# A new order of the same operations in a fused attention and feed-forward kernel

## The chip, the core and the metric

The kernel runs on one core of one Trainium2 chip. Its time is the device time of that core in microseconds (us), the median of several runs: 196.02 us before the change (three runs, 195.33 to 196.46). Apart from these runs one execution was profiled. It took 195.43 us, 193.5 us of it from the first to the last instruction (the span); the granted TensorE clock was 0.977 on average.

## What is computed

Two parts follow each other: an attention through 32 inducing points, and a feed-forward layer with x - tanh(x) in the middle.

```python
B, N, m, C = (4, 12480, 32, 128)
def mab(q, kv):
    s = scale * (q @ kv.transpose(0, 2, 1))
    s = s - s.max(-1, keepdims=True)
    a = np.exp(s)
    a /= a.sum(-1, keepdims=True) + 1e-09
    return a @ kv
h = mab(I, x)          # 32 inducing rows attend to the 12480 rows of a batch
x = mab(x, h)          # the 12480 rows attend to the 32 rows of h
...
h = x @ w_in           # 128 -> 2048
g = h - np.tanh(h)
return (g @ w_out).astype(np.float32)
```

All is float32. The output has 49920 rows of 128 numbers.

## The kernel before

**Tiling.** Each of the 4 batches is cut into 8 full segments of 1536 rows and one rest of 192 rows. A segment is written here as batch.segment, so 3.7 is the last full segment of the last batch and 3.8 is its rest. A full segment is 768 KB.

**First pass, for each batch.** The transposed segment is loaded (L383, `in_xT` into a `big` tile). TensorE multiplies it with the inducing rows (`scores`, L360 with `indT_sb`; called S1 here), and VectorE copies the scores out of PSUM and takes their maximum (L394). When all segments of a batch are through, the greatest score is found (L407 on VectorE, L409 on TensorE, L411, L417, and L420, which writes its negative `nbs`). Then comes, for each segment, the exponential on ScalarE (L468), a transpose of its 32x32 blocks on VectorE (L472, tile `et`), and the accumulation with the rows of x (L479; called ACC). ACC needs the segment with rows on the partitions. That layout comes in one of two ways: it is loaded from a second array (L462, `in_xn`), or, for the segments listed in `TURNED`, TensorE transposes it from the tile already there in three groups of four (L454; called T), and ScalarE or VectorE moves each group out of PSUM (L458). Batch 3 has two groups of segments (`GROUPS`): 3.0 and 3.1 are accumulated with a first greatest score, the others with the final one.

**Between the passes.** From the accumulated rows, `linear` works out for each batch the product with the two weight matrices to first order (L532, L356, L592), which leaves a small matrix `P_all` for each batch. A branch at the end goes to an exact form where the inputs are too large for this; it isn't taken here. The weights arrive as 64-bit words and are unpacked early in the program (L314 to L336: load, two steps on ScalarE, three on VectorE, two on GpSimd for each of 8 pieces).

**Second pass, for each segment.** S2 (L360 with `hT_all`) makes the scores, VectorE their maximum over 32 (L619, L620), ScalarE the exponential (L623), TensorE the product with `P_all` (L630; called prod). VectorE takes the sums out (L642) and inverts them (L645). The four quarters of the result leave PSUM either on VectorE, already scaled (L654), or on ScalarE unscaled (L658), after which GpSimd scales them in SBUF (L663). Then the segment is stored (L689). `DVQ` says how many quarters prefer VectorE.

**What sets the order.** No order is written by hand. `Plan.order` replays the list of operations with a cost for each, five engines and limited places: 23 `big` tiles, 8 PSUM banks and so on. An engine that is free takes the ready operation with the smallest priority number; the priorities are worked out from the table `K` (one number per batch and kind of operation, plus a step per segment). Each engine's instructions are then emitted in the order of this replay, and which tile an operation gets is settled by it too. At run time each engine takes its instructions strictly in that order. All DMAs, loads and stores, are issued by SyncE (SP) from one such queue, so a DMA that waits for its tile or its data holds back every DMA behind it. A load into a `big` tile waits until the last reader of that tile has finished: for a tile that held a transposed segment this is the segment's S2, for a tile with the other layout its ACC, for a result tile its store.

`LEAD`, `AHEAD`, `ISSUE` and `LAND` are the replay's DMA times, `SWITCH` and `STAY` its price for a change of TensorE mode, `MOST` limits how many `big` tiles one kind may hold.

Of the kernel before, what the change touches and what calls it, by code (L numbers as in the profile page):

```python
# [28 lines left out]
K = dict(load=(-307.0, -11.8, 121.4, 497.6), step1=(166.6, 10.8, 57.6, 54.7), lag2=(-1203.5, -373.8, -119.7, 417.3),
         copy=(-1617.1, 506.9, 485.8, -141.8), step2=(87.9, 64.9, 8.6, 29.9), turn=(1778.8, 1519.9, 3008.9, 2697.8),  # L30
         move=(-990.8, 721.0, 514.0, -475.8), nat=(-1233.4, 238.3, -127.2, -13.2), exp1=(-625.3, -464.9, 2706.6, 1215.5),
         et=(-962.3, 167.1, 1061.9, -1333.0), acc=(-504.7, 258.7, -313.0, -2258.1), sc2=(38.1, -215.7, -836.8, 1739.2),
         top=(1608.0, 619.3, 675.7, 692.4), exp2=(225.9, 24.6, 1508.1, -1683.1), prod=(-936.2, 1846.7, -190.5, 507.5),
         rec=(-1896.3, -404.8, 830.2, 246.0), ev=(1184.4, 55.1, 422.6, -1850.0), off=(-135.0, 428.4, 1368.7, 1417.9),
         step3=(99.8, 177.4, 103.4, 154.9), w1=-51.2, w2=1048.6, bound=2406.7)
# [868 lines left out]
```

## Time and profile before

| | |
|---|---|
| median of three runs | 196.02 us |
| the profiled execution | 195.43 us, of it 193.5 us span |
| TensorE (PE) busy | 159.4 us, 82% of the span |
| VectorE (DVE) busy | 149.1 us, 77% |
| ScalarE (ACT) busy | 113.0 us, 58% |
| GpSimd (POOL) busy | 96.8 us, 50% |
| moved by DMA | 67.26 MB, 41.17 MB read and 25.56 MB written |

In the profile's lines, PE stands for TensorE's matmuls and PEld for its weight loads. An L with a number is a line of the kernel. A group of instructions is written as engine, line, operation, output and input tile with shapes, and how many there were. A time in square brackets behind a row of the timeline is how long the engine stood idle just before it, and what it was released by; "issue" there means that it waited for nothing that the profile shows. A float32 matmul leaves two records, so an S1 or S2 of four matmuls counts as x8, an ACC as x24, a prod as x24; a group T of four transposes counts as x4.

### The profile page before, as it was taken

Reading aid. Unit: us, or ns where it says so; the run is one execution under the profiler, and the core shown is the slowest. Engines: PE = TensorE matmul, PEld = TensorE weight load, DVE = VectorE, ACT = ScalarE, POOL = GpSimd, SP = SyncE. Lnnn points to the kernel's source line nnn. Section 1 sums busy time; section 2 is a strip of 40 time slices with the busy share of each in tenths; the row PEclk is TensorE's granted clock in tenths of the full one; section 3 lists DMA queues with packets and bytes.
Section 4 is the critical chain, followed back from the end, with each engine's and each line's share of the span. In section 5 each row is a group of like instructions: output and inputs, shape, how many; then the busy total and the mean of one; then the engine's idle time right before and its main releaser. Section 6 shows DMA issues by size and latency. Waiting matters only on the chain.

```text
span 193.5 us, 7184 instructions
## 1 busy us (share of the span) xinstructions
PE 159.4 (82%) x2809; PEld 101.7 (53%) x2809; DVE 149.1 (77%) x556; ACT 113.0 (58%) x283; POOL 96.8 (50%) x117
## 2 busy tenths in 40 slices
PE   0799958686989969989999899997999996999500
PEld 0555647433466746546757675562776564565300
DVE  3277799979988858796799866993997679888950
ACT  3013399942289934766779924641797673588700
POOL 4000207645420547488544434432437995399980
PEclk9999999999999999999999999999999999999955
DMA  5999996999999999999999999999699995648893
GB/s 150 410 424 412 406 334 207 361 418 419 417 417 377 318 338 414 354 407 403 378 357 340 335 422 418 341 370 410 230 332 418 414 376 198 238 166 344 357 391 86
DMA packets 14201, 67.26 MB, mean 348 GB/s; under 512 B 1745, under 2 KB 2897, under 8 KB 14161
## 3 DMA queue, kind: packets, MB, share of 16 engines
q1 hardware_dynamic: 14160, 66.74, 90.2%
q8 instruction: 24, 0.39, 0.8%
q14 instruction: 17, 0.13, 0.2%
HBM read 41.17 MB, written 25.56 MB: 345 GB/s over the span
## 4 chain that ended last, share of the span: by engine, by line
PE 55%; DVE 13%; DMA 12%; ACT 8%; issue 5%; POOL 3%; SPq 0%; DVEq 0%; POOLq 0%; ACTq 0%
PE ps L360 17%; PE ps L630 13%; PE ps L454 10%; PE ps L479 8%; DMA big<-in_xT 7%; DMA big<-in_xn 5%; POOL big L663 3%; ACT ex L623 2%; ACT s L468 2%; PE ps L356 2%; ACT big L458 2%; ACT big L658 2%; PE ps L532 2%; DVE big L323 1%; DVE mb L619 1%
## 5 line engine op out<-in xcount | busy, mean ns | idle before, releaser
L663 POOL TENSOR_TENSOR big<-big,mb 128x384 f32<-128x384 f32 (+1 forms) x68 | 71.8, 1082 | 49.6 <-ACT big L658 41.0
L658 ACT COPY big<-ps 128x384 f32<-128x384 f32 x95 | 40.6, 491 | 10.8 <-DVE S_all L642 9.9
L630 PE MATMUL ps<-P_all,ex 32*128 32x129 f32 (+1 forms) x784 | 37.7, 292 | 3.1 <-issue 2.2
L630 PEld LDWEIGHTS ps<-P_all,ex 32*128 32x128 f32 (+1 forms) x784 | 29.5, 184 | 18.8 <-issue 8.0
L360 PE MATMUL ps<-big,indT_sb 128*32 128x384 f32 x256 | 27.7, 507 | 10.8 <-DMA big<-in_xT 8.3
L623 ACT ACTIVATE ex<-ps,mb 128x384 f32<-128x384 f32 (+1 forms) x36 | 20.2, 566 | 21.4 <-DVE mb L620 11.6
L458 ACT COPY big<-ps 128x512 f32<-128x512 f32 x30 | 17.3, 598 | 25.4 <-PE ps L454 24.9
L454 PE MATMUL ps<-ident,big 128*128 128x128 f32 x216 | 31.0, 288 | 0.0
L479 PE MATMUL ps<-big,et 128*32 128x128 f32 x768 | 27.0, 275 | 4.4 <-DVE et L472 3.1
L454 PEld LDWEIGHTS ps<-ident,big 128*128 128x128 f32 x216 | 24.2, 145 | 12.1 <-issue 5.3
L360 PE MATMUL ps<-big,hT_all 128*32 128x384 f32 x256 | 27.6, 491 | 1.5 <-issue 1.4
L479 PEld LDWEIGHTS ps<-big,et 128*32 128x32 f32 x768 | 20.8, 110 | 10.5 <-DVE et L472 5.1
L394 DVE TENSOR_SCALAR_CACHE_REDUCE s<-ps 128x384 f32<-128x384 f32 (+1 forms) x36 | 18.3, 518 | 10.1 <-PE ps L360 8.9
L642 DVE TENSOR_SCALAR S_all<-ps 128x3 f32<-128x3 f32 (+1 forms) x136 | 13.5, 154 | 10.7 <-PE ps L630 10.1
L619 DVE TENSOR_REDUCE mb<-ps 128x1 f32<-128x384 f32 (+1 forms) x36 | 18.4, 510 | 4.1 <-PE ps L360 3.6
L468 ACT ACTIVATE s<-s,nbs 128x384 f32<-128x384 f32 (+1 forms) x36 | 21.1, 608 | 0.0
L472 DVE STREAM_TRANSPOSE et<-s 128x384 f32<-128x384 f32 (+1 forms) x36 | 18.3, 525 | 1.6 <-ACT s L468 1.0
L458 DVE COPY big<-ps 128x512 f32<-128x512 f32 x24 | 16.4, 689 | 2.9 <-PE ps L454 2.5
L654 DVE TENSOR_TENSOR big<-ps,mb 128x384 f32<-128x384 f32 x33 | 17.6, 543 | 0.7 <-PE ps L360 0.2
L317 POOL TENSOR_SCALAR big<-big 128x512 f32<-128x512 f32 x8 | 5.3, 687 | 19.3 <-DMA big<-in_w_in 19.3
L360 PEld LDWEIGHTS ps<-big,indT_sb 128*32 128x32 f32 x256 | 6.1, 110 | 16.2 <-issue 7.5
L360 PEld LDWEIGHTS ps<-big,hT_all 128*32 128x32 f32 x256 | 6.9, 109 | 8.9 <-issue 5.1
(122 smaller groups left out, 159.4 us busy)
## 6 DMA issues: line engine op xcount, KB each, us to landing
big<-in_xT SPq DMA_DIRECT2D x32, 768.0 KB, 9.5
out<-big SPq DMA_DIRECT2D x30, 768.0 KB, 6.2
big<-in_xn SPq DMA_DIRECT2D x14, 768.0 KB, 9.3
big<-in_w_in SPq DMA_DIRECT2D x4, 512.0 KB, 12.8
big<-in_w_out SPq DMA_DIRECT2D x4, 512.0 KB, 10.3
out<-big SPq DMA_DIRECT2D x4, 384.0 KB, 3.1
xr<-in_xT SPq DMA_DIRECT2D x4, 96.0 KB, 8.8
xnr<-in_xl SPq DMA_DIRECT2D x4, 96.0 KB, 9.7
```

Source lines behind the costliest of these rows:

```text
L360: nc.tensor.matmul(ps[q * m:(q + 1) * m, :sg], lhsT=w, rhs=seg(x, nq, None, q), start=True, stop=stop)
L394: nc.vector.tensor_scalar(out=s1.get()[:P, :sg], in0=ps.get()[:P, :sg], scalar1=1.0, scalar2=None, op0=ALU.mult, op1=ALU.max, accum_out=mx ...
L454: nc.tensor.transpose(out=ps.get()[:, k * 128:(k + 1) * 128], in_=xt.get()[:, c:c + 128], identity=ident)
L458: copy(x.get()[:, 4 * g:4 * g + 4, :].rearrange("p k c -> p (k c)"), ps.get())
L468: nc.scalar.activation(out=t, in_=t, func=AF.Exp, bias=nbs.get()[:P, g:g + 1], accum_out=sums.get()[:P, s:s + 1])
L472: add("DVE", 0.5 if s < NS else 0.25, lambda et=et, s1=s1s[s], P=P, sg=sg, kb=kb: nc.vector.transpose(out=et.get()[:P, :kb].rearrange("p k ...
L479: nc.tensor.matmul(hacc.get()[q * m:(q + 1) * m, g * C:(g + 1) * C], lhsT=et.get()[:P, k, :], rhs=x.get()[:P, k, :], start=first_k[g, q] = ...
L619: nc.vector.tensor_reduce(out=mb.get()[:P, 0:1], in_=ps.get()[:P, :sg], axis=AX.X, op=ALU.max)
L623: add("ACT", 0.49 if full else 0.28, lambda: nc.scalar.activation(out=ex.get()[:P, :sg], in_=ps.get()[:P, :sg], func=AF.Exp, bias=mb.get() ...
L630: nc.tensor.matmul(o_b[q].get()[:T, r * (C + 1):(r + 1) * (C + 1)], lhsT=ex.get()[p, r * T:(r + 1) * T], rhs=P_all[p, b, :], start=True, s ...
L658: nc.scalar.copy(out=slot(q, q + 1), in_=o(q)[:, :, :C])
L663: nc.gpsimd.tensor_tensor(out=x, in0=x, in1=mb.get()[:T, 2 + q0 * nr:2 + q1 * nr].unsqueeze(2).to_broadcast([T, w, C]), op=ALU.mult)
```

## The change

Only numbers are changed, and one priority that was tied to another (`pri - 200`) becomes a number per batch in `K`.

```diff
-LEAD, AHEAD, ISSUE, LAND = 1.5, 4.0, 0.35, 1.5
-SWITCH, STAY = 0.115, 92.5
-MOST = dict(xT=15, xn=15, ot=21, pm=13)
-K = dict(load=(-307.0, -11.8, 121.4, 497.6), step1=(166.6, 10.8, 57.6, 54.7), lag2=(-1203.5, -373.8, -119.7, 417.3),
...
+LEAD, AHEAD, ISSUE, LAND = 1.50, 2.50, 0.35, 1.35
+SWITCH, STAY = 0.115, 138.5
+MOST = dict(xT=15, xn=14, ot=44, pm=24)
+K = dict(load=(-491.1, 150.9, 186.6, 689.9), step1=(131.5, 25.1, 45.2, 4.2), lag2=(-1155.7, -401.5, -325.5, 647.7),
...
-TURNED = ((0, 1, 2, 3, 4, 5, 6, 7), (2, 4, 6), (1, 2, 4, 5, 7), (4, 7))
+TURNED = ((0, 1, 2, 3, 4, 5, 6, 7), (1, 2, 4, 6), (1, 2, 4, 5, 7), (4,))
...
-DVQ = ((0, 3, 3, 1, 1, 2, 0, 0, 1), (0, 2, 1, 2, 1, 0, 1, 1, 1), (1, 0, 1, 3, 0, 0, 2, 1, 1), (2, 1, 2, 1, 2, 1, 2, 3, 0))
+DVQ = ((2, 3, 1, 2, 3, 1, 0, 2, 1), (1, 1, 2, 1, 0, 1, 0, 2, 1), (2, 0, 1, 3, 2, 0, 1, 1, 1), (1, 1, 2, 0, 0, 2, 2, 3, 0))
...
-                out=dst[:, q0 * nr:q1 * nr, :], in_=slot(q0, q1)), reads=[ot, *pieces[q0:q1]], pri=pri - 200)
+                out=dst[:, q0 * nr:q1 * nr, :], in_=slot(q0, q1)), reads=[ot, *pieces[q0:q1]], pri=pri + K["st"][b])
```

The count of operations of each kind on TensorE and of DMAs stays the same: 18 segments are transposed on TensorE before and after, and 14 are loaded in the second layout. One of them changes sides: 1.1 was loaded and is now transposed, 3.7 was transposed and is now loaded. Of the 136 quarters of the second pass, 31 instead of 33 full ones leave PSUM on VectorE and 97 instead of 95 on ScalarE, and GpSimd scales them in 70 instead of 68 pieces.

The first place is TensorE's row around the greatest score of batch 1, up to the first accumulation of that batch. Before, all transposes of batch 1 stand ahead of these rows; L409 and L417 are the greatest score's two steps, L592 and L356 belong to batch 0's `linear`, L360 is S1 of 2.0 and L479 the ACC of 1.0:

```order
L454 MATMUL ps_179<-ident,big_266 128x128 x4
L454 MATMUL ps_130<-ident,big_266 128x128 x4
L409 MATMUL ps_144<-ident,mx 1x128
L592 MATMUL ps_165<-wout_sb,W_627 32x128 x16
L417 MATMUL ps_137<-one,row 32x1 x4
L356 MATMUL ps_157<-P_753,foldx 32x128 x4
L360 MATMUL ps_172<-big_94,indT_sb 32x384 x4
L479 MATMUL ps_144<-big_252,et_372 32x128 x12
```

The same place now:

```order
L409 MATMUL ps_149<-ident,mx 1x128
L454 MATMUL ps_142<-ident,big_226 128x128 x4
L454 MATMUL ps_128<-ident,big_282 128x128 x4
L592 MATMUL ps_170<-wout_sb,W_631 32x128 x16
L417 MATMUL ps_177<-one,row 32x1 x4
L360 MATMUL ps_149<-big_86,indT_sb 32x384 x4
L454 MATMUL ps_135<-ident,big_282 128x128 x4
L356 MATMUL ps_157<-P_759,foldx 32x128 x4
L454 MATMUL ps_142<-ident,big_282 128x128 x4
L479 MATMUL ps_128<-big_338,et_372 32x128 x12
```

Four of the transposes (the last group of 1.4 and the three of 1.6) moved behind the start of the search for the greatest score, between its steps; the three groups of 1.1 are new and stand further ahead.

The second place is SP's row where batch 3's second layout is loaded. Before, xn 3.0 and 3.1 come first, then xT 3.7, then the stores of 1.3 to 1.5, then xn 3.2, 3.3, 3.5, 3.6 and the rest's, then stores again:

```order
L462 DMA big_177<-in_xn 128x1536
L462 DMA big_252<-in_xn 128x1536
L383 DMA big_94<-in_xT 128x1536
L689 DMA out<-big_266 128x1536
L689 DMA out<-big_226 128x1536
L689 DMA out<-big_342 128x1536
L462 DMA big_252<-in_xn 128x1536
L462 DMA big_266<-in_xn 128x1536
L462 DMA big_336<-in_xn 128x1536
L462 DMA big_342<-in_xn 128x1536
L462 DMA xnr_308<-in_xl 64x384
L689 DMA out<-big_319 128x1536
```

The same place now, from xT 3.7 on: xn 3.0, the store of 1.4, then xn 3.1, 3.2, 3.3, 3.5, 3.6 and 3.7 in a row, the rest's, and only then the store of 1.5:

```order
L383 DMA big_252<-in_xT 128x1536
L462 DMA big_86<-in_xn 128x1536
L689 DMA out<-big_126 128x1536
L462 DMA big_313<-in_xn 128x1536
L462 DMA big_133<-in_xn 128x1536
L462 DMA big_126<-in_xn 128x1536
L462 DMA big_155<-in_xn 128x1536
L462 DMA big_349<-in_xn 128x1536
L462 DMA big_133<-in_xn 128x1536
L462 DMA xnr_769<-in_xl 64x384
L689 DMA out<-big_200 128x1536
```

The loads of xn 3.0 and 3.1 moved behind xT 3.7, xn 3.7 is new and takes the tile that xn 3.2 had (`big_133`), and the store of 1.5 moved behind them all. By the tiles that they take, xn 3.0 now waits for S2 of 2.0, 3.1 for S2 of 2.1, 3.2 for S2 of 2.2, 3.3 for the store of 1.4, 3.5 for S2 of 2.3, 3.6 for S2 of 2.4 and 3.7 for ACC of 3.2.

The third place is VectorE's row between batch 3's final greatest score (L420) and the first block transpose that depends on it (L472, segment 3.2). Before, with two of the moves of 3.7 (L458) between them:

```order
L420 TENSOR_SCALAR nbs<-ps_172 128x1
L458 COPY big_226<-ps_157 128x512
L425 TENSOR_REDUCE nmx<-nbs 128x1
L458 COPY big_226<-ps_144 128x512
L472 STREAM_TRANSPOSE et_389<-s_142 128x384
```

Now:

```order
L420 TENSOR_SCALAR nbs<-ps_142 128x1
L645 RECIPROCAL mb_741<-S_all 128x12
L425 TENSOR_REDUCE nmx<-nbs 128x1
L654 TENSOR_TENSOR big_313<-ps_177,mb_741 128x384
L472 STREAM_TRANSPOSE et_410<-s_140 128x384
```

The two moves are gone, and a reciprocal and one quarter of 2.1 stand there instead.

From L532 of batch 3 (the start of its `linear`) to the end of the program TensorE has the same operations in the same order before and after, but for two pairs of rows that change places; GpSimd has the same from L582 of batch 3 on.

More of the change, by code (lines that the diff above doesn't have):

```diff
@@ L25 @@
 SMALL = 0.0625
-LEAD, AHEAD, ISSUE, LAND = 1.5, 4.0, 0.35, 1.5
-SWITCH, STAY = 0.115, 92.5
-MOST = dict(xT=15, xn=15, ot=21, pm=13)
-K = dict(load=(-307.0, -11.8, 121.4, 497.6), step1=(166.6, 10.8, 57.6, 54.7), lag2=(-1203.5, -373.8, -119.7, 417.3),
[L30 to L35, printed above, removed]
-TURNED = ((0, 1, 2, 3, 4, 5, 6, 7), (2, 4, 6), (1, 2, 4, 5, 7), (4, 7))
+LEAD, AHEAD, ISSUE, LAND = 1.50, 2.50, 0.35, 1.35
+SWITCH, STAY = 0.115, 138.5
+MOST = dict(xT=15, xn=14, ot=44, pm=24)
+K = dict(load=(-491.1, 150.9, 186.6, 689.9), step1=(131.5, 25.1, 45.2, 4.2), lag2=(-1155.7, -401.5, -325.5, 647.7),
+         copy=(-1436.1, -91.7, 401.2, 866.6), step2=(53.0, 21.8, 29.6, 11.2), turn=(2464.2, 1619.9, 3834.7, 2397.6),
+         move=(-1235.8, 1620.0, 792.5, -1062.6), nat=(-88.4, 388.6, 263.4, 221.6), exp1=(-761.0, -1191.3, 3121.8, 1092.9),
+         et=(-1743.8, -396.7, 697.9, -989.9), acc=(-415.6, 311.0, -914.8, -2852.2), sc2=(397.9, -270.3, -981.4, 1175.3),
+         top=(1314.2, 389.7, 382.8, 391.6), exp2=(699.1, 100.5, 1581.4, -1536.3), prod=(-1389.7, 1876.4, 309.4, 838.7),
+         rec=(-1614.8, -1055.1, 943.4, 458.0), ev=(1578.9, 169.1, 83.6, -1972.7), off=(-434.6, 597.2, 1423.8, 1605.1),
+         step3=(98.7, 160.5, 133.8, 209.3), st=(-638.4, -255.5, -294.7, 320.5), w1=-629.9, w2=752.2, bound=2143.0)
+TURNED = ((0, 1, 2, 3, 4, 5, 6, 7), (1, 2, 4, 6), (1, 2, 4, 5, 7), (4,))
 GROUPS = ((0,), (0,), (0,), (0, 2))
-DVQ = ((0, 3, 3, 1, 1, 2, 0, 0, 1), (0, 2, 1, 2, 1, 0, 1, 1, 1), (1, 0, 1, 3, 0, 0, 2, 1, 1), (2, 1, 2, 1, 2, 1, 2, 3, 0))
+DVQ = ((2, 3, 1, 2, 3, 1, 0, 2, 1), (1, 1, 2, 1, 0, 1, 0, 2, 1), (2, 0, 1, 3, 2, 0, 1, 1, 1), (1, 1, 2, 0, 0, 2, 2, 3, 0))
 LOADED = [(b, s) for b in range(4) for s in range(8) if s not in TURNED[b]]
```

## The prediction

> **What bounds the kernel now.** I read the page first, for the shares (the table above), then the stretches, to see where each engine fills, then the timeline of TensorE and VectorE at the stretches that aren't full, then how long DMAs took from issue to landing.
>
> ```profile
> core 0: us, PE busy (x) PEld busy (x) DVE busy (x) ACT busy (x) POOL busy (x), PEclk, DMA share, GB/s
> 24.00:30.00 6.00, 3.24 (x45) 2.60 (x46) 5.88 (x17) 5.38 (x13) 1.34 (x2) 1.00 0.86 291
> 42.00:48.00 6.00, 4.70 (x72) 2.19 (x68) 5.76 (x18) 1.61 (x4) 2.59 (x2) 1.00 1.02 421
> 48.00:54.00 6.00, 5.61 (x55) 2.44 (x56) 5.93 (x18) 1.67 (x3) 2.50 (x3) 1.00 1.01 414
> 96.00:108.00 12.00, 12.00 (x210) 7.90 (x206) 11.07 (x41) 10.13 (x29) 5.28 (x5) 1.00 0.99 329
> 138.00:145.00 7.00, 6.94 (x144) 5.29 (x147) 6.58 (x23) 6.56 (x22) 3.63 (x3) 1.00 0.85 268
> ```
>
> No engine bounds the whole. TensorE has the most work, 82% of the span, but from 24 to 54 us VectorE is the full one (5.88, 5.76 and 5.93 of 6 us) while TensorE waits, and from 42 to 54 us the DMAs run at their highest rate too, 414 to 421 GB/s. From 96 to 108 us TensorE is full while DMA gives only 329 GB/s. A new order removes no work, so it can win only where TensorE stands idle and has work that could be moved there, or lose where a load comes too late.
>
> One part can be set aside. From L532 of batch 3 on the order is the same, and that stretch is long:
>
> ```profile
> 154.17 1.39 PE L532 MATMUL ps<-win_sb,hT_all 128*32 128x512 f32 x8
> ```
>
> 193.5 - 154.2 = 39.3 us. So the change has to act ahead of 154 us, and I count its terms as shifts of this L532. The prices of TensorE's pieces come from the chain and the timeline:
>
> ```profile
> 11.18 1.46 PE ps L454 x12
> 60.19 0.88 PE ps L630 x24
> 61.86 0.65 PE ps L360 x8
> 62.50 0.65 PE ps L479 x24
> 86.95 0.87 PE ps L592 x32
> 88.70 0.36 PE ps L356 x8
> 98.15 0.31 PE ps L409 x2
> 54.42 1.57 ACT big L458 x3
> ```
>
> So a transposed segment is 1.46 us on TensorE, a prod 0.88, an S1 or S2 0.65, an ACC 0.65; the two parts of `linear` are 0.87 and 0.36, the steps of a search for the greatest score about 0.3. Moving a transposed segment out costs ScalarE 1.57.
>
> **Term 1: 1.1 is transposed, 3.7 is loaded.** Up to L532 of batch 3 TensorE's sum stays the same; 1.46 us move from after 136 us to before 59 us. What matters is whether they fit into idle time there.
>
> ```profile
> 51.13 0.85 PE L360 MATMUL ps<-big,indT_sb 128*32 128x384 f32 x8 [0.19 <-DVE wout_sb L332]
> 52.94 0.85 PE L360 MATMUL ps<-big,indT_sb 128*32 128x384 f32 x8
> 58.10 0.43 PE L356 MATMUL ps<-P,foldx 128*32 128x128 f32 x8 [0.76 <-ACT P L595]
> 59.32 0.86 PE L479 MATMUL ps<-big,et 128*32 128x128 f32 x24 [0.15 <-DVE et L472]
> ```
>
> S1 of 1.6 starts at 51.13 and S1 of 1.7 at 52.94. The load of 1.7 took this long:
>
> ```profile
> 34.30 5.01 SPq L383 DMA_DIRECT2D big<-in_xT  x4
> big<-in_xT SPq DMA_DIRECT2D x1, 768.0 KB, 13.5
> ```
>
> It was the last of those four, issued at about 39.0, and landed at 52.5, right before its S1. At 418 GB/s (between the rates above) 768 KB are 1.9 us, and in the new row of SP the load of xn 1.0 no longer stands ahead of the xT of batch 1. So 1.7 can land about 1.9 us earlier, at 50.6. Of the new row between S1 of 1.7 and ACC of 1.0, TensorE has 9 groups of transposes (9 x 1.46 / 3 = 4.4 us), the two parts of `linear` (1.2), S1 of 2.0 (0.65) and the search's steps (0.3), 6.6 us, and I count 7 for the changes between them. From an end of S1 at about 51.5 this is done at 58.5, ahead of 59.32. And ACC of 1.0 waits for the search and the exponential, which hang on VectorE:
>
> ```profile
> 55.24 0.12 DVE L407 TENSOR_REDUCE mx<-mxg 128x1 f32<-128x9 f32 x1
> 57.56 0.16 DVE L420 TENSOR_SCALAR nbs<-ps 128x1 f32<-128x1 f32 x1
> ```
>
> VectorE has the same work ahead of L420 in both orders (L407 goes ahead of one maximum, the others stay), so L420 and the ACC come at about the same time, but by then TensorE has done the transposes of 1.1 on top of all that stood ahead of this ACC before. If it fits, the term is -1.46 us. If 1.7 lands no earlier, the row ends at 53.7 + 7.0 = 60.7, 59.32 is passed by 1.3 us, and the term is -0.2. I take -1.2, since the DMA rate there is steady. The moves of 1.1 are all ScalarE's, which is busy only 1.6 of 6 us there; without that cover they would add 1.57 us.
>
> **Term 2: xT 3.0.** TensorE waited for it:
>
> ```profile
> 101.19 9.62 DMA big<-in_xT
> 110.94 0.85 PE L360 MATMUL ps<-big,indT_sb 128*32 128x384 f32 x8 [0.87 <-DMA big<-in_xT]
> ```
>
> It is issued when S2 of 1.5 has freed its tile. Before, 8.1 us of TensorE's work (six groups T, four ACC, two prod, one S2 and the same S1) lay between that S2 and S1 of 3.0; now it is 6.3 us (five ACC, two prod, one group T, one S2 and the rest's small S1). The load itself now follows the other DMAs around it by some 4 us more, and 96 to 108 us had DMA to spare, so it should take less than 9.62 us. At the 7.4 us of a load that stood alone in SP's row (123.43, below) TensorE waits 1.1 us, 0.2 more than now. Bounds: -0.9 (covered) and +2.4 (9.6 us, less 6.3 and 0.9). I take +0.2.
>
> ```profile
> 123.43 0.33 SPq L383 DMA_DIRECT2D big<-in_xT  x1
> big<-in_xT SPq DMA_DIRECT2D x1, 768.0 KB, 7.4
> 130.55 8.22 SPq L462 DMA_DIRECT2D big<-in_xn  x4
> big<-in_xn SPq DMA_DIRECT2D x3, 768.0 KB, 7.2
> 1.20 4.65 DMA big<-in_xT
> ```
>
> **Term 3: xn 3.1 to 3.7 just in time.** By the new tiles, the work on TensorE between what frees a tile and the ACC that needs the load is 5.0 us for 3.1 (one S1, two S2, two prod, one ACC, 0.36 and 0.3), 5.5 for 3.2, 6.7 for 3.5, 5.1 for 3.6 and 5.8 for 3.7. Loads took 7.2 us in this stretch, while stores were under way, and 4.65 us at the start, when nothing else was. In the new row no store stands among them, so the lower row is the nearer one; but they follow each other by 1.9 us on the wire. Six loads from S2 of 2.1 on are 11.3 us, plus 2.8 (4.65 - 1.9) until the last lands, 14.1 us, against 13.7 us of work to ACC of 3.7. So a wait of 0.4 us at the best and, at 7.2 us each, of about 2.2 (7.2 - 5.0) once, since they are pipelined and the wait isn't paid six times. What is queued behind them on SP: the stores of 1.5, 2.0, 1.6, 2.1 and 1.7, five times 1.9 us; 138 to 145 us gave 268 GB/s, so there is room. I take +0.5.
>
> [...]
>
> **Term 4: the moves of 3.7 go.**
>
> ```profile
> 139.21 0.15 DVE L420 TENSOR_SCALAR nbs<-ps 128x1 f32<-128x1 f32 x1
> 139.33 0.69 DVE L458 COPY big<-ps 128x512 f32<-128x512 f32 x1
> 140.00 0.68 DVE L458 COPY big<-ps 128x512 f32<-128x512 f32 x1
> 140.59 1.03 DVE L472 STREAM_TRANSPOSE et<-s 128x384 f32<-128x384 f32 x2
> 141.22 1.52 PE L479 MATMUL ps<-big,et 128*32 128x128 f32 x48
> L654 DVE TENSOR_TENSOR big<-ps,mb 128x384 f32<-128x384 f32 x33 | 17.6, 543 | 0.7 <-PE ps L360 0.2
> L645 DVE RECIPROCAL mb<-S_all 128x12 f32<-128x12 f32 x32 | 7.0, 220 | 1.3
> ```
>
> Two moves of 0.69 us stood between L420 and the first block transpose, and ACC of 3.2 started when it was done. Now 0.22 + 0.54 stand there: 1.37 - 0.76 = 0.6 us earlier, if the load of 3.2 is there; if not, 0. I take -0.6.
>
> **The rest.** Two quarters leave VectorE: -2 x 0.54 there, +2 x 0.49 on ScalarE, +2 x 0.83 on GpSimd, which is idle half of the span; its last stretch is unchanged. I cost that at 0.
>
> ```profile
> L658 ACT COPY big<-ps 128x384 f32<-128x384 f32 x95 | 40.6, 491 | 10.8 <-DVE S_all L642 9.9 <-PE ps L360 0.2 <-issue 0.2
> L663 POOL TENSOR_TENSOR big<-big,mb 128x384 f32<-128x384 f32 x41 | 33.3, 827 | 3.6 <-ACT big L658 2.8 <-DVE et L472 0.9
> 134.63 0.84 PE L360 MATMUL ps<-big,hT_all 128*32 128x384 f32 x3 [1.39 <-issue]
> ```
>
> TensorE also stands still in the middle of an S2 (five records before, three behind) for 1.39 us with nothing to wait for; a new order can lengthen or shorten such halts, and I put 1.0 us either way into the range.
>
> **The sum.** -1.2 + 0.2 + 0.5 - 0.6 = -1.1 us. The profiled execution would go from 195.43 to 194.3, and as the median lay 0.59 us above it, I forecast 194.9 us, 0.6% less.
>
> **The rivals.** (a) Loads too late, slower: if loads take as long as in the present trace, term 2 is +2.4, term 3 +2.2 and term 4 is 0; with term 1 that is +3.4 us, 199.4, and with term 1 and half of the two +1.1, 197.1. It decides once loads take more than about 6.5 us after the freeing S2. For it speak the 7.2 and 9.62 us; against it that fewer DMAs stand around them. Chance 0.24. (b) The gain of term 1 is given back: VectorE, full from 24 to 54 us and 11.07 of 12 us from 96 on, sets the pace, and TensorE's lead of 1.4 us only becomes longer waits for it: 0.2 + 0.5 - 0.6 = +0.1, 196.1, and 195.5 if half of term 1 stays. Chance 0.31. (c) More is won: terms 1 and 4 in full, the 0.87 us of term 2 gone and a halt of 1.39 us gone: -1.46 - 0.6 - 0.9 + 0.4 - 1.39 = -4.0, 192.0. Chance 0.10. The forecast itself, between about 193 and 195, has 0.35.
>
> **The chances.** A measurement of this kernel can tell about 0.5%, 1.0 us, from no change. Faster is the forecast and (c), 0.45; within it is (b), 0.31; slower is (a), 0.24. The range leaves out the far halves of (a) and (c): 192.4 to 198.0.
>
> **What would show it.** Right: ACC of 1.0 still at about 59 us with the 1.6 transposes done; L532 of batch 3 at about 153.1 instead of 154.17; from there 39.3 us to the end. Wrong: TensorE waiting on DMA ahead of an ACC of batch 3 for over 1 us; S1 of 3.0 waiting over 2 us; or a last stretch that isn't 39.3 us, which I have held fixed.

## The result, and the profile after

The new order took 191.65 us (median of 4 runs, 188.98 to 193.10) against 196.08 us of the kernel before on the same chip: a ratio of 0.968, 95% interval 0.960 to 0.976. An identical kernel run again took 191.77 us, ratio 0.980 (0.973 to 0.988). The medians are of all runs; the ratios leave out, on both sides, the runs that were more than 1.5% above the fastest one of their kernel. So the change gains 2 to 3%; forecast were 194.9 us, and the range ended at 192.4. The profiled execution of the new order took 193.1 us, 191.3 of it span. It is the longest of the four, so below it is read for its places and not for its sum.

The stretches of the new order, in the columns of those of before:

```profile
core 0: us, PE busy (x) PEld busy (x) DVE busy (x) ACT busy (x) POOL busy (x), PEclk, DMA share, GB/s
48.00:54.00 6.00, 5.63 (x58) 3.19 (x55) 5.93 (x20) 1.89 (x4) 2.13 (x4) 1.00 1.01 413
96.00:108.00 12.00, 12.00 (x260) 9.38 (x256) 11.09 (x42) 11.35 (x33) 6.57 (x6) 1.00 0.97 327
138.00:145.00 7.00, 4.69 (x134) 3.60 (x137) 4.03 (x21) 3.94 (x11) 4.66 (x5) 1.00 1.02 402
145.60:149.00 3.40, 3.40 (x55) 2.37 (x48) 1.80 (x8) 1.56 (x4) 0.04 (x1) 0.50 1.02 422
```

From 96 to 108 us little changed, 12.00 us of TensorE and 327 GB/s. From 138 to 145 us TensorE is busy only 4.69 us where it was 6.94. And from 145.6 to 149.0 us the granted clock is 0.50; no such stretch stood there before.

TensorE's timeline of the new order at the places that the prediction named (S1 of 1.7, ACC of 1.0, S1 of 3.0, ACC of 3.2 and 3.3, L532 of batch 3) and around them, with the greatest score of batch 3 (L409):

```profile
50.38 0.85 PE L360 MATMUL ps<-big,indT_sb 128*32 128x384 f32 x8
...
58.97 0.86 PE L479 MATMUL ps<-big,et 128*32 128x128 f32 x24
...
107.89 0.85 PE L360 MATMUL ps<-big,indT_sb 128*32 128x384 f32 x8
...
110.39 0.52 PE L479 MATMUL ps<-big,et 128*32 128x128 f32 x10 [1.22 <-issue]
...
130.48 0.27 PE L409 MATMUL ps<-ident,mx 128*1 128x128 f32 x1
...
136.04 0.86 PE L479 MATMUL ps<-big,et 128*32 128x128 f32 x24 [0.74 <-DMA big<-in_xn]
137.92 0.86 PE L479 MATMUL ps<-big,et 128*32 128x128 f32 x24 [1.02 <-DMA big<-in_xn]
...
144.44 0.75 PE L479 MATMUL ps<-big,et 128*32 128x128 f32 x19 [2.31 <-issue]
...
146.07 1.67 PE L630 MATMUL ps<-P_all,ex 32*128 32x129 f32 x24
147.67 1.50 PE L479 MATMUL ps<-big,et 128*32 128x128 f32 x24
...
152.12 1.34 PE L532 MATMUL ps<-win_sb,hT_all 128*32 128x512 f32 x8 [0.54 <-DVE mb L645]
```

S1 of 1.7 starts 2.6 us earlier (52.94 before), ACC of 1.0 at the old time (59.32) with the transposes of 1.1 done, and S1 of 3.0 no longer waits. L532 of batch 3 comes 2.05 us earlier (154.17), and from there to the end of the span it is 39.2 us (39.3 before). Two things stand out. The loads of 3.2 and 3.3 come late, by 1.76 us together. And TensorE halts twice in the middle of an ACC, for 1.22 and 2.31 us, with nothing to wait for ("issue"); the halts of before at other places are gone, the 1.39 us in S2 of 2.2 and this one in prod of 0.2, shown here from the timeline of before with its greatest score of batch 3:

```profile
69.88 0.72 PE L630 MATMUL ps<-P_all,ex 32*128 32x129 f32 x15 [1.51 <-issue]
...
136.87 0.38 PE L409 MATMUL ps<-ident,mx 128*1 128x128 f32 x2
```

So the new order was 6.4 us ahead at the greatest score of batch 3 and had lost 4.3 us of that again at L532; the halt of 2.31 us and the late loads lie in between.

I had put such halts into the range with 1.0 us either way. The experiments are about them first, and then about the terms.

### The profile page after: what moved, and what is told of

Its sections match the earlier page's. It is cut to its first block, busy times and chain, and to the rows that moved or that the text cites. A ratio compares the mean times of both kernels' runs of the same rounds, so it can differ in the third digit from the quotient of the medians.

```text
span 191.3 us, 7198 instructions
## 1 busy us (share of the span) xinstructions
PE 157.8 (82%) x2809; PEld 104.3 (55%) x2809; DVE 149.2 (78%) x556; ACT 112.2 (59%) x283; POOL 98.3 (51%) x119
## 5 line engine op out<-in xcount | busy, mean ns | idle before, releaser
L663 POOL TENSOR_TENSOR big<-big,mb 128x384 f32<-128x384 f32 (+1 forms) x70 | 73.4, 1076 | 46.9 <-ACT big L658 37.9
L630 PE MATMUL ps<-P_all,ex 32*128 32x129 f32 (+1 forms) x784 | 36.4, 295 | 0.8 <-ACT ex L623 0.5
L479 PE MATMUL ps<-big,et 128*32 128x128 f32 x768 | 30.0, 289 | 8.2 <-issue 3.5
L360 PE MATMUL ps<-big,indT_sb 128*32 128x384 f32 x256 | 27.4, 504 | 10.2 <-DMA big<-in_xT 8.1
L458 ACT COPY big<-ps 128x512 f32<-128x512 f32 x30 | 16.9, 591 | 27.2 <-PE ps L454 27.1
L479 PEld LDWEIGHTS ps<-big,et 128*32 128x32 f32 x768 | 23.4, 115 | 13.7 <-issue 6.4
L454 PE MATMUL ps<-ident,big 128*128 128x128 f32 x216 | 30.1, 285 | 0.2 <-ACT big L458 0.2
L360 PE MATMUL ps<-big,hT_all 128*32 128x384 f32 x256 | 27.4, 492 | 0.0
L619 DVE TENSOR_REDUCE mb<-ps 128x1 f32<-128x384 f32 (+1 forms) x36 | 18.3, 509 | 5.7 <-PE ps L360 5.3
L472 DVE STREAM_TRANSPOSE et<-s 128x384 f32<-128x384 f32 (+1 forms) x36 | 18.5, 527 | 2.0 <-ACT big L658 1.2
L458 DVE COPY big<-ps 128x512 f32<-128x512 f32 x24 | 16.3, 686 | 2.3 <-PE ps L454 1.8
L654 DVE TENSOR_TENSOR big<-ps,mb 128x384 f32<-128x384 f32 x31 | 16.5, 542 | 0.5
L360 PEld LDWEIGHTS ps<-big,indT_sb 128*32 128x32 f32 x256 | 6.4, 109 | 17.5 <-issue 7.7
L360 PEld LDWEIGHTS ps<-big,hT_all 128*32 128x32 f32 x256 | 7.9, 109 | 4.4 <-issue 1.5
```

What stands on the lines that cost most here:

```text
L360: nc.tensor.matmul(ps[q * m:(q + 1) * m, :sg], lhsT=w, rhs=seg(x, nq, None, q), start=True, stop=stop)
L454: nc.tensor.transpose(out=ps.get()[:, k * 128:(k + 1) * 128], in_=xt.get()[:, c:c + 128], identity=ident)
L458: copy(x.get()[:, 4 * g:4 * g + 4, :].rearrange("p k c -> p (k c)"), ps.get())
L472: add("DVE", 0.5 if s < NS else 0.25, lambda et=et, s1=s1s[s], P=P, sg=sg, kb=kb: nc.vector.transpose(out=et.get()[:P, :kb].rearrange("p k ...
L479: nc.tensor.matmul(hacc.get()[q * m:(q + 1) * m, g * C:(g + 1) * C], lhsT=et.get()[:P, k, :], rhs=x.get()[:P, k, :], start=first_k[g, q] = ...
L619: nc.vector.tensor_reduce(out=mb.get()[:P, 0:1], in_=ps.get()[:P, :sg], axis=AX.X, op=ALU.max)
```

## The experiments

Times are compared with runs of the kernel before on the same chip; its median there was 194.9 to 196.2 us.

### Where the halts come from

My theory was that a halt is TensorE running out of code. Instructions are fetched during the run, through a DMA queue of their own: in the trace of before its fetches begin from 20.47 to 192.74 us. The page of before lists it beside the data:

```profile
q1 hardware_dynamic: 14160, 66.74, 90.2%
q8 instruction: 24, 0.39, 0.8%
```

That is 24 fetches of 16 KB for 2 x 2,809 records of TensorE. In the trace's records of this queue a fetch ends shortly ahead of each long halt's end: one from 67.40 to 68.43 us, and TensorE goes on at 69.88; in the new order one from 141.94 to 143.12 us, and TensorE goes on at 144.44. The records of all 19 profiles say more than these two. There are 35 halts marked "issue" of 0.2 us and over between 20 us and L532 of batch 3, and each ends 1.25 to 1.61 us after a fetch has ended. Counted over all of TensorE's records, those of its sequencer too, each also stands just ahead of a record whose number is 193 plus a multiple of 256: TensorE halts where a new block of code begins. So a block is 256 records here, one fetch of 16 KB, and of the 17 blocks that begin in this stretch of the new order's first profile two have such a halt.

To move the code without changing the order, I gave TensorE small matmuls that feed nothing: 32 of them are 128 records, half a block. They run at the start, while TensorE waits for the first load. All engines' orders stay as they were.

```diff
-    add("POOL", 0.6, lambda: make_identity(nc, ident), writes=[ident_b], pri=-10)
+    ident_b.first = add("POOL", 0.6, lambda: make_identity(nc, ident), writes=[ident_b], pri=-10)
...
         op.fn()
+        if op is ident_b.first: [nc.tensor.matmul(home(ps_p, "ps", 7, [128, 512])[:32, :1], lhsT=ident[:, :32], rhs=ident[:, :1], start=True, stop=True) for _ in range(32)]
```

**The new order again, and both orders moved by half a block** (three kernels). On record for the first:

> The changed kernel once more, unaltered. Theory A (the order itself removes waits: the work of 1.1 in idle time, no wait at S1 of 3.0, less before the ACCs of batch 3): the gain over the kernel before stays at 2.5 to 4%, and L532 of batch 3 starts 2 to 6 us ahead of the old 154.2 us in any profile of it, with about 39 us behind it. Theory B (the gain is where TensorE's unexplained halts in mid-instruction fall, 1.5 and 1.4 us before, 1.2 and 2.3 us now): the halts sit at other places or have other lengths in a second profile, and the times spread by as much as the halts, 2 to 4 us. Theory C (the granted clock: two stretches of 3.4 us at half clock in the first profile, none in the old kernel's): a profile without them is 2 to 3 us shorter.

For the new order moved:

> The changed kernel with 32 tiny matmuls (128 records) on TensorE in the idle time before the first load lands; they feed nothing. Every later instruction of TensorE stands 128 places further back in its code. Theory B (halts come where TensorE's code is fetched in blocks of 256 instructions, 24 fetches of 16 KB in the instruction queue): the halts move to other instructions, and the time moves by up to 2 us either way. Theory A: time within 1% of the unshifted kernel, and the milestones up to the first halt the same within 0.3 us.

For the old order moved:

> The kernel before with the same 32 tiny matmuls. Theory B: the halts of 1.51 us in prod of 0.2 and of 1.39 us in S2 of 2.2 move or go, and the time moves by up to 3 us, in the extreme to the changed kernel's. Theory A: 196 us within 1%.

Measured: 191.77 us again; the new order moved 188.84 us (188.31 to 189.51, ratio 0.970, 0.963 to 0.977); the old order moved 190.42 us (188.62 to 194.54, ratio 0.977, 0.967 to 0.987). So 32 matmuls that compute nothing make the old kernel 2.3% faster, which is most of what the change gained. In the profiles of both moved kernels, each of the shortest run of its kernel, no halt of TensorE over 0.2 us is left between 20 us and L532 of batch 3. First the old order moved (S1 of 1.7, the greatest score of batch 3, the one wait for a load late in the first pass, L532 of batch 3):

```profile
52.67 0.85 PE L360 MATMUL ps<-big,indT_sb 128*32 128x384 f32 x8
...
130.78 0.38 PE L409 MATMUL ps<-ident,mx 128*1 128x128 f32 x2
...
136.50 0.86 PE L479 MATMUL ps<-big,et 128*32 128x128 f32 x24 [0.47 <-DMA big<-in_xn]
...
147.49 1.04 PE L532 MATMUL ps<-win_sb,hT_all 128*32 128x512 f32 x8
```

Then the new order moved, at the same places:

```profile
50.67 0.85 PE L360 MATMUL ps<-big,indT_sb 128*32 128x384 f32 x8 [0.18 <-DVE wout_sb L332]
...
59.27 0.86 PE L479 MATMUL ps<-big,et 128*32 128x128 f32 x24
...
129.52 0.27 PE L409 MATMUL ps<-ident,mx 128*1 128x128 f32 x1
...
132.13 0.86 PE L479 MATMUL ps<-big,et 128*32 128x128 f32 x24 [0.46 <-DMA big<-in_xn]
...
137.51 0.86 PE L479 MATMUL ps<-big,et 128*32 128x128 f32 x24 [2.15 <-DMA big<-in_xn]
...
147.84 1.07 PE L532 MATMUL ps<-win_sb,hT_all 128*32 128x512 f32 x8 [0.54 <-DVE mb L645]
```

The old order's L532 of batch 3 goes from 154.17 to 147.49 us by the move alone. Its greatest score of batch 3 comes 1.26 us later than the new order's, 130.78 against 129.52, but at L532 it is 0.35 us ahead. The spans are 186.7 and 186.4 us: in these two runs without halts the two orders are nearly alike.

The kernel run again unaltered has one halt in its profile, 1.79 us at 144.90 us, in the same ACC as the 2.31 us; the halt of 1.22 us is gone. The stretch of half clock behind the large halt is gone too, but the run took 193.18 us, so the 2 to 3 us of theory C in the first expectation don't show.

**A whole block** (64 small matmuls) puts every instruction at its old place within a block again. If the added work did the good and not the place, it should stay fast. The second 32 stand ahead of ACC of 0.0, where TensorE is idle:

```diff
             def acc(et=et, x=x, s=s, P=P, kb=kb, g=g0):
+                for _ in range(32 if (b, s) == (0, 0) else 0):
+                    nc.tensor.matmul(hacc.get()[:32, 300:301], lhsT=ident[:, :32], rhs=ident[:, :1], start=True, stop=True)
```

On record for the old order, for the new, and for the old with the second 32 alone:

> The order of before with 64 small matmuls added (256 TensorE records, 32 matmuls at the start and 32 in TensorE's idle time ahead of ACC of 0.0), so that TensorE's code is moved by a whole block of a code fetch instead of half a block. Theory A (the halts depend on where in a block the code lies when DMA is crowded): the halts of 1.51 and 1.39 us near 68 and 133 us come back and the time is that of before, 195.5 us, ratio 0.995 to 1.005. Rival B (the added work itself, early on, brings the gain of the half block): no halts, 190.4 us, ratio 0.97 to 0.98.

> The new order with the same 64 small matmuls. Theory A: a halt of 1.2 to 2.3 us comes back near 108 or 143 us and the time is that of the new order, 191.7 us, ratio 0.975 to 0.985. Rival B: as with half a block, 188.8 us, ratio 0.965 to 0.972.

> The order of before with only the 32 small matmuls in TensorE's idle time ahead of ACC of 0.0 (half a block, from 27 us on). Theory A: the halts at 68 and 133 us are gone, 190.4 us, ratio 0.97 to 0.98. Rival B (only work at the very start matters): 195.5 us, ratio 0.995 to 1.005.

Measured: 195.45 us for the old order (193.81 to 197.66, ratio 1.006, 1.001 to 1.011) and 192.48 for the new (189.84 to 194.87, ratio 0.985, 0.975 to 0.995). Both are back, so it is the place. The old order's timeline, moved by a whole block, has halts in prods again:

```profile
69.17 0.72 PE L632 MATMUL ps<-P_all,ex 32*128 32x129 f32 x15 [0.95 <-issue]
...
77.11 0.82 PE L632 MATMUL ps<-P_all,ex 32*128 32x129 f32 x18 [1.31 <-issue]
...
119.77 0.71 PE L632 MATMUL ps<-P_all,ex 32*128 32x129 f32 x12 [1.44 <-issue]
```

The first stands where 1.51 us stood in before, after the same nine records of that prod (x15 are left); the second where before had 0.21 (76.72 us, also x18). All four halts of this profile stand at a place in the code where before had one, 1.51, 0.21, 0.46 and 0.27 us then and 0.95, 1.31, 1.44 and 0.46 now; the one in S2 of 2.2 did not come back. The new order's large halt came back in the same ACC, with 19 records left as at 144.44:

```profile
146.25 0.75 PE L481 MATMUL ps<-big,et 128*32 128x128 f32 x19 [3.14 <-issue]
```

Counted in the trace, 4545 records of TensorE (matmuls, weight loads and its sequencer's) stand ahead of the start of that fetch in the new order and 4801 here, the 256 added ones more. Half a block that comes late, at 27 us, gave 191.66 us (190.44 to 192.87, ratio 0.990, 0.979 to 1.000) and halts of 0.55 and 0.22 us only. By the halts this is near to the half block at the start, by the ratio nearer to none than to that, and the interval touches 1: neither theory gave it.

**A quarter and three quarters** (16 small matmuls at the start; 32 there and 16 ahead of ACC of 0.0):

> The order of before moved by a quarter of a block (16 small matmuls at the start). Theory A (halts by where the code lies): a time between the 190.4 us of half a block and the 195.5 us of none. Theory C (only half a block is special): 195.5 us.

> The new order moved by a quarter of a block. Theory A, in which the order's own worth is that of its terms, about 1.5 us, and the rest is where its code lies: 1 to 2.5 us below the quarter block of the old order in the mean over the four places (0, 1/4, 1/2, 3/4). Theory B (the order itself is worth all that was measured): 3.5 to 4.4 us below at each place. Theory D (the order itself is worth nothing): within 0.7 us in the mean.

> The order of before moved by three quarters of a block (32 small matmuls at the start, 16 ahead of ACC of 0.0). Theory A: between 190.4 and 195.5 us. Theory C: 195.5 us.

> The new order moved by three quarters of a block. Theory A: in the mean over the four places 1 to 2.5 us below the old order. Theory B: 3.5 to 4.4 us below it at this place too. Theory D: within 0.7 us in the mean.

With these, each order stands at four places in a block. Ratios are to the kernel before on the same chip, halts are the sum of those of 0.2 us and over between 20 us and L532 of batch 3, in the one profile:

| moved by | old: median, ratio | halts | L532 of b. 3 | new: median, ratio | halts | L532 of b. 3 |
|---|---|---|---|---|---|---|
| 0 | 196.08, 1 | 3.84 | 154.17 | 191.65, 0.968 (0.960 to 0.976) | 3.53 | 152.12 |
| 0, again | | | | 191.77, 0.980 (0.973 to 0.988) | 1.79 | 151.03 |
| 1/4 | 195.83, 0.998 (0.992 to 1.004) | 2.01 | 151.07 | 189.59, 0.974 (0.967 to 0.982) | 1.34 | 148.02 |
| 1/2 | 190.42, 0.977 (0.967 to 0.987) | 0 | 147.49 | 188.84, 0.970 (0.963 to 0.977) | 0 | 147.84 |
| 3/4 | 192.34, 0.989 (0.981 to 0.996) | 0.49 | 150.01 | 192.27, 0.980 (0.972 to 0.989) | 4.00 | 151.52 |
| 1 | 195.45, 1.006 (1.001 to 1.011) | 4.16 | 154.24 | 192.48, 0.985 (0.975 to 0.995) | 4.10 | 153.93 |

Each profile is of one run. Those of the new order at 0, 3/4 and 1 are of runs above the median of their kernels, those at 1/2 of the shortest, so the columns of halts tell what a run can have and not the mean.

By the ratios the new order is ahead by 2.6% (mean of the two), 2.4, 0.7 and 0.8% at the four places: 1.6% in the mean, 3.2 us, with a standard error of 0.5% by the scatter of the four. The last two, each with an interval of about 1.2% either way, can't be told from nothing by themselves. So the theory of 3.5 to 4.4 us at every place falls, and so, in the mean, does that of no worth at all; I had expected 1 to 2.5 us, of which only the upper end lies within that error (1.0 us). Every microsecond of halts goes with about 1.4 us of L532 (a line through the six profiles of the old order, the late half block among them; 1.3 through the six of the new), so a halt seems to cost more than itself. One part of that is below under the clock; but the kernel before, with 3.84 us of halts and no half clock behind them, comes to L532 6.7 us later than moved by half a block, so the rest stays open.

**Fewer bytes of stores.** Why is the code late? Either the fetch waits behind data, or the place alone makes it late. First try:

```diff
             add("SP", (2.12 if full else 0.35) * (q1 - q0) / nq, lambda q0=q0, q1=q1: nc.sync.dma_start(
-                out=dst[:, q0 * nr:q1 * nr, :], in_=slot(q0, q1)), reads=[ot, *pieces[q0:q1]], pri=pri - 200)
+                out=dst[:, q0 * nr:(q0 + 1 if b < B - 1 else q1) * nr, :], in_=slot(q0, q0 + 1 if b < B - 1 else q1)), reads=[ot, *pieces[q0:q1]], pri=pri - 200)
```

> The order of before, its code where it was, with the stores of batches 0 to 2 cut to their first quarter (three quarters of those rows of the output are left out), so that the DMA queues are shorter and nothing else is changed on TensorE. Theory A (TensorE halts when a code fetch waits behind data in a crowded DMA queue): no halt over 0.3 us between 60 and 154 us, and L532 of batch 3 at 146 to 149 us instead of 154.17. Rival B (a halt belongs to the place in the code, however busy DMA is): the halts of 1.51 and 1.39 us in prod of 0.2 and S2 of 2.2 stay.

> The new order, its code where it was, with the same stores cut. Theory A: no halt over 0.3 us between 60 and 154 us, L532 of batch 3 at 145 to 148 us instead of 152.12, and 0.5 to 2 us ahead of that of the old order cut in the same way, which is then the order's own worth. Rival B: the halt of 2.31 us near 143 us stays. Rival D (without halts the two orders are alike): L532 of batch 3 within 0.5 us of that of the old order.

Measured: 190.82 us for the old order (ratio 0.972, 0.965 to 0.979) and 192.26 for the new (0.971, 0.963 to 0.980), L532 of batch 3 at 151.26 and 151.32: by ratio and place the two orders are alike here. A large halt stayed in each, 1.77 us at 70.95 and 2.89 us at 143.91, which looks like the rival. It doesn't settle it, though. The new order's halt and the stretch of DMA that it lies in:

```profile
143.91 1.29 PE L479 MATMUL ps<-big,et 128*32 128x128 f32 x19 [2.89 <-issue]
```

```profile
core 0: us, PE busy (x) PEld busy (x) DVE busy (x) ACT busy (x) POOL busy (x), PEclk, DMA share, GB/s
139.00:144.00 5.00, 2.11 (x62) 1.56 (x66) 2.83 (x19) 2.24 (x5) 3.94 (x5) 0.92 1.00 358
```

DMA was still full there, 1.00 and 358 GB/s: with less to store, loads and later stores had moved together.

**DMA nearly idle at the place.** So the next pair cut the stores of batches 0 to 2 to a twelfth and left out the late loads of xn as well (in the new order 3.1 to 3.3 and 3.5 to 3.7), with the code unmoved:

```diff
-                add("SP", 2.0 if s < NS else 0.3, lambda x=x, s=s: nc.sync.dma_start(
+                if (b, s) == (3, 0): x0 = x
+                if (b, s) in ((3, 1), (3, 2), (3, 3), (3, 5), (3, 6), (3, 7)): x.make = lambda n: x0.get()
+                add("SP", 2.0 if s < NS else 0.3, lambda x=x, s=s: (b, s) in ((3, 1), (3, 2), (3, 3), (3, 5), (3, 6), (3, 7)) or nc.sync.dma_start(
```

> The order of before, its code where it was, with much less DMA late in the program: the stores of batches 0 to 2 are cut to a twelfth, and the loads of xn 3.1, 3.2, 3.3, 3.5 and 3.6 are left out (their ACC read the tile of xn 3.0). Theory A (a code fetch waits behind data): from 110 us on, where DMA has little to do, no halt over 0.3 us. Rival B (a halt belongs to the place in the code): the halts in prod of 0.2 near 68 us and S2 of 2.2 near 130 us stay, 1.3 to 1.8 us each.

> The new order, its code where it was, with the same stores cut to a twelfth and the loads of xn 3.1 to 3.3 and 3.5 to 3.7 left out, so that DMA has little to do from about 125 to 150 us, where the halt of 2 to 3 us came in four profiles (between ACC of 3.6 and S2 of 2.6). Theory A (a code fetch waits behind data): that halt is gone or below 0.3 us. Rival B (a halt belongs to the place in the code): it stays, 1.5 us or longer, at the same place in TensorE's row.

Measured: 189.87 us for the old order (ratio 0.973, 0.968 to 0.978) and 186.42 for the new (0.954, 0.946 to 0.961). The new order's stretches (with the 1.24 us halt at 70.61 in the first of them), and its timeline where the large halt had been:

```profile
core 0: us, PE busy (x) PEld busy (x) DVE busy (x) ACT busy (x) POOL busy (x), PEclk, DMA share, GB/s
66.00:72.00 6.00, 4.76 (x126) 3.46 (x121) 3.98 (x17) 3.87 (x7) 4.02 (x5) 1.00 0.70 243
...
138.00:145.00 7.00, 7.00 (x198) 5.02 (x190) 6.33 (x32) 5.58 (x17) 4.61 (x5) 1.00 0.17 47
```

```profile
70.61 0.41 PE L481 MATMUL ps<-big,et 128*32 128x128 f32 x4 [1.24 <-issue]
...
141.47 0.84 PE L481 MATMUL ps<-big,et 128*32 128x128 f32 x23
142.09 0.86 PE L360 MATMUL ps<-big,hT_all 128*32 128x384 f32 x8
142.88 0.95 PE L632 MATMUL ps<-P_all,ex 32*128 32x129 f32 x24
147.57 1.06 PE L534 MATMUL ps<-win_sb,hT_all 128*32 128x512 f32 x8 [0.54 <-DVE mb L647]
```

With DMA 17% busy the ACC runs through, x23 in 0.84 us, TensorE fills 7.00 of 7 us, and no halt of 0.2 us or over marked "issue" stands from 72 us to the L532 here (line 534 in this kernel). A wait of 0.35 us at 117.55, put down to VectorE, also stands at the first record of a block, with DMA full. The old order so treated has none from 72 us on either; its L532 comes at 149.17 us, 1.6 us behind the new order's, which has one load fewer. Both keep one halt near 70 us, 1.22 and 1.24 us, where DMA is still 70 to 84% busy. The fetch that had started after 4545 records now starts after 4294. So it takes both: a place in the code, and a busy DMA (a share of 1.02 from 138 to 145 us in the new order and 0.17 here; 0.70 and 0.84 at the two halts near 70 us).

The same records tell what makes a place prone. A block's fetch begins about when TensorE passes the first record of the block ahead of it, or later: between 60 and 150 us 0.80 to 6.50 us later in the traces of before and of the new order. In that stretch it took 0.9 to 1.3 us in nearly all cases (2.0 at most), whether DMA was full or not; its start is what differs. In the new order TensorE passed record 4289 at 136.29 us, and the fetch began 5.65 us later, took 1.18 us, and TensorE went on 1.32 us after it; that is 8.15 us, and TensorE had done its 256 records in 5.84. With DMA nearly idle the fetch began 0.03 us after that record (136.88 and 136.91). So TensorE halts where it gets through a block faster than the next one comes. Half a block isn't a cure by itself: four blocks of the moved new order came just in time, 1.35 to 1.59 us ahead of their use. Why a fetch waits nearly 6 us at one place of a full DMA and under 1 us at another stays open.

### The terms

**The loads of 3.2 and 3.3 left out**, in the new order moved by half a block, to see whether its waits of 0.46 and 2.15 us lie on the path:

```diff
+            elif (b, s) in ((3, 2), (3, 3)):
+                add("SP", 2.0, lambda: None, reads=[xT_b[b, s]], writes=[x], pri=q0 + K["nat"][b])
+                x.make = lambda n: x0.get()
```

> The new order moved by half a block (188.84 us), without the loads of xn 3.2 and 3.3: their ACC reads the tile of xn 3.0, so two of 14 loads of xn are left out. Theory A (the waits for loads of batch 3, 2.6 us in that kernel, lie on the path): the wait of 2.15 us ahead of ACC of 3.3 is gone, L532 of batch 3 comes at 145.5 to 146.2 us instead of 147.84, and the time is 186.5 to 187.2 us. Rival B (another wait takes its place, VectorE's block transposes L472 or the loads of xn 3.5 to 3.7): L532 of batch 3 within 0.5 us of 147.84 and 188.3 to 188.9 us.

Measured: 189.48 us (188.29 to 191.41, ratio 0.979, 0.971 to 0.987) against 188.84 with the loads, so no gain. Its timeline at ACC of 3.3, ACC of 3.7 and L532:

```profile
135.96 0.86 PE L484 MATMUL ps<-big,et 128*32 128x128 f32 x24 [0.25 <-DVE et L477]
...
143.04 1.33 PE L484 MATMUL ps<-big,et 128*32 128x128 f32 x24 [0.61 <-DMA big<-in_xn]
...
147.33 1.07 PE L537 MATMUL ps<-win_sb,hT_all 128*32 128x512 f32 x8 [0.54 <-DVE mb L650]
```

From the greatest score of batch 3 (the first of its last two L409) to L532 it takes 17.2 us (130.10 to 147.33) instead of 18.3 (129.52 to 147.84). So in one profile of each 1.1 us of the 2.15 that went were on the path; VectorE's `et` and the load of 3.7 took the rest. At L532 0.5 us of that is left, as a halt of 1.33 us at 113.28 us, new in this kernel, stands ahead of the greatest score, and at the end nothing (a span of 186.4 us in both). Of the two theories the one of another wait in its place is the nearer.

**Term 1 undone**, also on the new order moved by half a block: in SP's row xn 1.0 changes places with xT 1.4 to 1.7, tiles included, so that it stands ahead of them as before. The five operations and their tiles turn by one step after planning:

```diff
-    for op in plan.order():
+    done = plan.order()
+    ring = [row_sp[1, 4, "xT"], row_sp[1, 5, "xT"], row_sp[1, 6, "xT"], row_sp[1, 7, "xT"], row_sp[1, 0, "xn"]]
...
+    for op in done:
```

> The new order moved by half a block (188.84 us, no halts), with one part of the change undone: in SP's row the load of xn 1.0 stands ahead of xT 1.4 to 1.7 again, as before; all other rows are those of the new order. Theory A (term 1 comes from 1.7 landing earlier): S1 of 1.7 goes from about 50.4 back to about 52.5 us, ACC of 1.0 0.5 to 2 us later than the 58.9 us of the new order, and as much at L409 of batch 2. Rival B (the transposes of 1.1 fit in anyway, xn 1.0's place is worth nothing): S1 of 1.7 later, but ACC of 1.0 and L409 of batch 2 within 0.3 us of those of the new order.

```profile
50.81 0.85 PE L360 MATMUL ps<-big,indT_sb 128*32 128x384 f32 x8 [1.09 <-DMA big<-in_xT]
...
52.70 0.85 PE L360 MATMUL ps<-big,indT_sb 128*32 128x384 f32 x8 [0.39 <-DMA big<-in_xT]
...
61.29 0.86 PE L479 MATMUL ps<-big,et 128*32 128x128 f32 x24
```

S1 of 1.7 is back at 52.70, with waits for xT that the new order doesn't have. ACC of 1.0 comes at 61.29 instead of 59.27, 2.0 us later, and L409 of batch 2 is still 1.6 later (97.19 against 95.58). The time is 190.79 us (189.35 to 193.51, ratio 0.971, 0.965 to 0.978): above 188.84, but by ratios the two cannot be told apart. The places in the trace decide for the theory, at the upper end of what it gave.

**The priority of stores**, the one number per batch that is new in `K`, set back to -200 in the new table; the planner then works out another order from it:

> The changed kernel with the priority of the stores put back to -200 for every batch. The planner then gives another order on every engine. Theory A with the stores' place as a cause of its own: slower by 1 to 3 us than the changed kernel. If the gain is elsewhere (loads and transposes): within 1% of it. A planner that was tuned as a whole can also lose more than 3 us by one number.

```profile
111.41 0.52 PE L479 MATMUL ps<-big,et 128*32 128x128 f32 x10 [1.63 <-issue]
...
141.15 0.86 PE L479 MATMUL ps<-big,et 128*32 128x128 f32 x24 [1.38 <-DMA big<-in_xn]
145.05 0.86 PE L479 MATMUL ps<-big,et 128*32 128x128 f32 x24 [1.98 <-DMA big<-in_xn]
151.35 1.06 PE L532 MATMUL ps<-win_sb,hT_all 128*32 128x512 f32 x8 [0.29 <-DVE hT_all L517]
```

193.48 us (191.37 to 198.84, ratio 0.991, 0.985 to 0.996): slower than the new order. In its profile TensorE waits 3.7 us for loads of xn in batch 3 (1.8 in the new order), and it has a halt of its own. Since code and halts move with such an edit too, the 1.7 us between them cannot be put down to the loads alone.

No kernel here that does all its work had a lower median than the new order moved by half a block, 188.84 us, 0.970 of before.

## Why the prediction was wrong

**The step that failed** is the one on halts: "a new order can lengthen or shorten such halts, and I put 1.0 us either way into the range". The halts were worth several times that. Moving the code by half a block, with no change of order, takes 2.3% (4.5 us) off the old order; off the new one it takes 0.4%, the mean of its two ratios at place 0 (0.974) against 0.970. Moved so, with no halts in the profile of either, the new order is ahead by 0.7% (0.977 against 0.970). So of 2.6%, the mean gain of the two runs, 0.7 is order and 1.9, or 3.7 us, is that the old order stood badly and the new one less so; by the intervals of the ratios each part is known to about 1.3% either way. In single profiles that isn't to be seen in the sum of halts (3.84 against 3.53 and 1.79): executions of one kernel differ by up to 6 us (192.93 to 199.11 for the old order moved by a quarter), so this split rests on the timed runs. It was rival (c), "a halt of 1.39 us gone", that came nearest with 192.0 us. That it came so near is partly luck, as it also needed term 4 in full, which wasn't there. I gave it 0.10, counted one halt of the several in my own trace, and didn't count what follows a halt.

**Term 1 (-1.2) was right.** ACC of 1.0 at the same time as before with 1.46 us more done: 58.97 against 59.32, and 59.27 against 59.04 in the moved pair. It does rest on 1.7 landing earlier, as the undone part shows (its S1 is 2.0 us earlier in the moved pair; 1.9 were forecast).

**Term 2 (+0.2) was about right, on a load that varies.** In three profiles of the new order S1 of 3.0 starts 0.13 us after its load has landed, so the load decides. It took 6.63 us in the first, 8.58 in the second and 7.44 in the moved kernel, where 7.4 were forecast; ahead of S1 TensorE was idle for under 0.15, 1.95 and 0.80 us, against 0.87 before and 1.1 forecast. The profile puts the latter two down to ScalarE, as here in the second:

```profile
111.10 0.85 PE L360 MATMUL ps<-big,indT_sb 128*32 128x384 f32 x8 [1.95 <-ACT big L658]
```

In the moved pair the greatest score of batch 3, which stands behind terms 1 and 2, came 1.26 us earlier (that of batch 2 only 0.5); forecast were 1.0.

**Term 3 (+0.5) was too small, and term 4 (-0.6) wasn't there.** The waits for xn 3.1 to 3.7 were 1.76 us in the new order, 1.45 in its second profile and 2.6 in the moved one (0.47 in the old order moved), near the +2.2 that I had as the far bound; the cover on TensorE that I counted (5.0 to 6.7 us) was too short, because these loads took 5.5 to 8.6 us from issue to landing in the moved kernel, 7.5 in the middle. The 4.65 us that I took for a load alone was that of the first of eight issued in 4.4 us. Term 4 held only "if the load of 3.2 is there". In VectorE's row the block transposes do follow L420 of batch 3 sooner:

```profile
132.84 0.14 DVE L420 TENSOR_SCALAR nbs<-ps 128x1 f32<-128x1 f32 x1
...
133.82 0.57 DVE L472 STREAM_TRANSPOSE et<-s 128x384 f32<-128x384 f32 x1
```

0.98 us after it instead of 1.38, but ACC of 3.2 then waits for its load until 136.04. Between the greatest score and L532 the moved pair loses 1.6 us (-1.26 becomes +0.35), where terms 3 and 4 together were -0.1. This loss belongs to both; it was not taken apart further than by the two loads left out, which give 1.1 of it, in one profile of each.

**The stretch held fixed** was fixed in these two profiles, 39.2 us against 39.3; in the second profile of the new order it took 40.3 and in the moved pair 38.6 against 39.2, so it is steady to about 1 us and no better. **The rest, put at 0,** shows no cost: GpSimd is busy 98.3 us instead of 96.8, off the path.

That the forecast of 0.6% lies by the 0.7% of the moved pair is luck. At L532, where its terms act, that pair has the new order 0.35 us behind and not 1.1 ahead, since terms 3 and 4 were off by 1.7 us, and a ratio there is known to about 1.2% only. Left open: the mean over four places is 1.6%, more than the terms and the halts in the profiles explain.

## What to carry to other kernels

Before a gain or loss of a few per cent is put down to a new order, move the code by half a block (128 records here) with instructions that do nothing, for both kernels: if that alone moves the time as much, as here with 2.3% off the old order, the comparison tells of the place of the code. A halt with "issue" on TensorE in the middle of an operation, 1.2 to 2.3 us each for the four largest in the first two profiles, is a term of the sum and not noise for the range. Where DMA is full, small matmuls at the start can be tried against it, at several counts: here 32 left no halt in the profile of either order, and 48 left 4.0 us in the new one's. And a load that takes the tile of an operation 5 us ahead of its use is late where loads take 7, as here with waits of 2.6 us for xn in the moved new order.

## What was not expected of the hardware

**Half the clock behind some halts.** Behind the halt of 2.31 us the granted clock was 0.50 for 3.4 us, and a prod took 1.67 us instead of 0.95, an ACC 1.50 instead of 0.86. The same behind the 3.14 us in the new order moved by a whole block:

```profile
147.50:150.90 3.40, 3.40 (x52) 2.36 (x48) 1.83 (x8) 1.58 (x4) 0.07 (x1) 0.52 1.03 424
```

and, with no halt but a wait of 2.03 us for the load of 3.3 ahead of it, in the kernel with term 1 undone:

```profile
139.30:142.70 3.40, 3.40 (x55) 2.37 (x48) 1.79 (x4) 2.26 (x7) 2.25 (x2) 0.52 1.00 339
```

3.4 us at half the clock are up to 1.7 us of work. A halt of 1.44 us in the old order moved by a whole block was followed by such a stretch too, from 120.87 us on (a clock of 0.55 in the mean from 120.5 to 123.9 us). But the wait of 2.15 us in the new order moved by half a block, and the 1.51 and 1.39 us of before, were followed by nothing of the kind. The two such stretches of the new order's first profile, from 29.56 and from 145.61 us, are 3.41 us long each. Ahead of the four told of here TensorE had been idle for 1.4 to 3.1 us. Why the same wait is sometimes followed by one and sometimes not is not shown.

**Early work on TensorE didn't help its start.** The small matmuls at 1.37 us do not bring the first greatest score forward: L409 of batch 0 stands at 25.29 us in the new order moved by half a block and at 24.58 and 25.26 in the two profiles of the new order itself.
